# Fused gated-recurrence and feed-forward kernel: first groups of two blocks, one more y transpose by DMA, last output split at column 288, new instruction orders

## The chip, the cores and the metric

The kernel runs on one core of one Trainium2 chip. The metric is the device time of one execution in microseconds. Ten runs of the kernel before gave a median of 182.35 us, from 181.86 to 183.18.

## What is computed

Two stages follow each other. The first is a gated linear recurrence for 4 batches, 8 heads, 768 steps and a head width of 48; its output is laid out as 3072 tokens of 384 values. The second is a feed-forward layer with 2048 hidden values and a squared ReLU.

```python
for t in range(S):
    state = alpha[:, :, t, :, None] * state + np.einsum('bhd,bhe->bhde', k[:, :, t], v[:, :, t])
    y[:, :, t] = np.einsum('bhd,bhde->bhe', q[:, :, t], state)
x = y.transpose(0, 2, 1, 3).reshape(B * S, H * D)
r = np.maximum(x @ w_in, 0.0)
out = (s * (r * r) + b) @ w_out
```

Inputs and output are float32; the kernel multiplies in bfloat16 and accumulates in float32.

## The kernel before

**Blocks.** The tokens are cut into 24 blocks of 128 steps, six for each batch. Within a block the recurrence is written as matrix products. The logarithm of alpha is summed over the steps on TensorE ("cum", L533 for blocks 0 to 5, L766 for later ones), and its exponentials scale q and k (exp on ScalarE, L558 or L781; products on VectorE, L601 and L609, or L801). The scaled q and k are transposed: blocks 0 to 12 on TensorE (L619, L812) with a copy out of PSUM (L629 and L631, L822 and L824), later ones by a DMA transpose (L827). The transposed q and k give the products A of queries with keys (L711), which a mask on VectorE makes causal (L725). "KV" products of k and v (L647, L835) feed the running state: VectorE adds (L679), GpSimd multiplies by the block's decay (L686, `st_snew`); for block 0 ScalarE copies the product first (L673, `st_scopy`). Block y is the sum of state and q (L742) and of masked A and v (L750); ScalarE takes it out of PSUM (L848).

Blocks 0 to 5 are worked as three pairs with the two steps of a pair of rows side by side (`pair_ops`, L1024); for pairs 0 and 1 a selection product on TensorE brings v into order (L577, copies L588 and L590), for pair 2 four DMAs do (L596). Later blocks are worked one by one (`block_ops`, L1125). v is cast to bfloat16 by ScalarE or GpSimd, as lists at the top of the file say (L571 or L573, L796 or L798).

**Feed-forward.** y is transposed, on TensorE (L853) with a copy (L865, L867) or by a DMA transpose (L870), and the blocks are gathered in groups by `GROUPS`. For every group, `mm1` (L884) multiplies the transposed y by w_in, always into a full bank of 128 x 512 values: four column blocks of the hidden layer for a group of one block, two for a group of two, one for a group of four. ScalarE takes the ReLU (L900), VectorE squares (L912). `mm2` (L919) multiplies the squares by w_out, four products to an operation, sixteen to a block of the output. The output is scaled by s and gets its bias from VectorE in one operation (L934), for the first six blocks from ScalarE and GpSimd (L951, L958), and is stored from SP's queue (L945). The last block's output is worked in two halves of columns, each with its own products, evacuation and store (`half_of`, L914). w_in and w_out arrive in quarters of 768 KB in four buffers, which they share (L442, L456), and are cast in halves by GpSimd or ScalarE (L451 and L453, L465 and L467); w_out's quarter waits until w_in's has been cast.

**The order.** No engine's order follows the program text. Every operation is recorded with a duration and its dependencies (`op`, L131), and `ORDER` holds a list of operation numbers for each engine, which were found by a search beforehand. `Schedule.run` (L156) goes through these lists with the recorded durations, gives out the six PSUM banks on the way and yields begin times; `emit` (L240) writes the operations in this order of time. It also puts dummy products on zeros (L1201) ahead of a TensorE operation that is planned to come after a gap, in the first 36 us. The planner lets GpSimd and VectorE begin after their constants:

```python
free = {e: {"POOL": 6.9, "DVE": 4.5}.get(e, 0.7) for e in engines}
```

The engines run their lists strictly in order, so an operation that waits holds all that stand behind it on its engine. Loads and stores all go through SP's queue, in SP's order.

Of the kernel before, what the change touches and what calls it, by code (L numbers as in the profile page):

```python
# [13 lines left out]
GROUPS = [1, 1, 2, 2, 2, 4, 2, 2, 2, 2, 4]  # L14
# [6 lines left out]
POOL_CASTS = [0, 1, 2, 5, 6]  # L21
CASTP = -400.0
W_HW = True
WIN_CASTS = [0, 1, 2, 5, 6]
A2 = [0, 1, 2, 5, 8, 9, 10]
POOL_V = [2]
ACT_V1 = [6, 8, 9, 13, 15, 17, 22, 23]
ACT_T1 = [7, 8]
DVE_VC = [3]
DVE_YC = [2, 3, 4, 7, 10, 13]  # L30
NIN = 4
PE_T = [6, 7, 8, 9, 10, 11, 12]
PE_Y = [7, 8, 9, 10, 11, 13]
# [3 lines left out]
ACT_T = [2, 3]  # L37
# [3 lines left out]
NOUT = 4  # L41

# [4 lines left out]
        31 35 32 33 34 36 37 38 0 3 6 9 39 12 41 16 42 40 21 43 26 47 213 45 52 44 353 46 375  # L47
        397 49 48 50 354 355 356 51 377 413 376 378 510 298 414 399 398 415 400 587 512 114 530
        416 513 663 511 607 532 533 589 590 678 531 736 133 609 610 541 588 666 210 665 608 598
        203 618 826 750 680 529 679 811 738 664 739 275 282 689 752 674 753 871 681 346 851 626  # L50
        737 606 814 352 813 751 497 491 747 761 828 829 699 853 694 854 827 812 852 873 503 837
        822 872 774 509 862 769 882 580 874 845 586 850 870 887 656 735 662 804 729 810 941 947
        959 953 965
    """,
    "POOL": """
        81 1 2 4 83 8 158 10 14 160 13 17 212 23 27 232 303 53 310 368 113 390 405 412 421 202
        518 209 132 595 274 544 601 281 621 671 744 677 758 764 819 834 825 840 865
    """,
    "ACT": """
        57 134 66 67 68 69 144 146 70 147 58 143 145 60 62 80 135 153 155 87 93 137 89 95 5 7 97  # L60
        164 11 100 103 211 170 116 106 122 219 217 221 119 174 218 220 125 180 18 177 186 183
        192 22 283 189 28 285 195 299 286 301 112 236 131 242 302 357 287 379 244 359 360 401
        382 381 249 246 403 404 307 201 208 255 361 252 261 297 365 417 258 314 383 267 420 419
        514 372 264 517 321 374 318 516 327 591 324 394 273 534 330 593 594 333 536 537 396 429
        339 435 611 667 336 437 538 614 669 613 670 442 682 439 448 445 528 740 280 451 454 615
        457 685 460 742 743 684 463 548 466 469 472 475 478 830 754 481 605 484 625 832 815 757
        555 756 833 552 818 561 817 558 567 564 875 573 686 693 855 698 570 857 858 631 628 877
        634 637 640 878 643 646 773 649 859 768 704 701 710 707 716 713 722 719 849 844 779 879
        869 776 785 782 886 788 791 794 797 889 892 895 898 901 904 907 910 913 916 919 922 925
        928 931 934  # L70
    """,
    "DVE": """
        71 72 73 74 76 149 78 150 148 151 91 85 90 82 139 168 162 167 157 98 159 101 104 166 117
        172 107 123 15 120 175 225 126 224 181 178 223 187 222 229 19 184 231 227 20 190 234 239
        193 240 289 288 24 196 238 25 291 29 293 305 304 295 250 247 30 362 54 363 309 256 312
        253 385 262 384 367 56 370 316 389 259 387 268 422 407 265 406 322 423 392 319 409 425
        411 325 520 328 427 433 432 334 331 519 524 431 540 340 522 337 597 543 526 443 440 539
        600 449 446 617 452 455 620 596 546 458 673 461 616 464 467 676 351 345 550 603 470 473
        476 623 479 687 688 485 482 672 746 496 556 490 749 553 760 562 559 568 696 691 565 695
        574 763 502 745 508 821 632 571 759 629 824 635 579 638 641 585 836 644 771 770 766 861  # L80
        647 839 650 835 705 820 864 702 711 860 708 881 655 717 714 880 842 846 847 720 661 723
        867 780 884 728 777 786 783 789 792 795 734 798 890 893 896 899 902 905 908 911 809 914
        917 920 923 926 929 932 803 935 940 958 946 952 964
    """,
    "PE": """
        63 64 65 141 142 140 75 77 59 61 79 84 152 154 138 86 92 161 136 88 94 156 96 163 99 102
        115 169 165 105 121 171 215 216 214 118 173 176 124 179 108 182 185 191 109 228 127 128
        230 226 188 129 284 194 233 110 111 130 300 197 235 198 241 204 237 205 290 206 243 292
        358 199 380 294 248 245 402 200 306 207 308 296 254 311 251 260 364 366 257 55 313 266
        369 418 386 315 388 263 269 371 515 270 320 373 391 317 271 326 408 424 323 410 393 272  # L90
        329 592 426 332 535 276 277 395 428 338 523 434 335 430 278 436 521 612 668 279 441 542
        525 438 444 599 447 341 527 342 450 683 453 741 343 456 344 619 459 545 347 348 462 465
        547 349 675 350 549 471 468 602 477 474 492 480 604 622 486 483 831 487 755 624 493 488
        554 551 494 495 489 816 498 748 560 499 557 500 566 563 690 504 505 572 506 762 692 501
# [171 lines left out]
def kernel(  # L266
# [22 lines left out]
    d_model = moe_w_in.shape[0]  # L289
# [584 lines left out]
    for g, m in enumerate(GROUPS):  # L874
# [3 lines left out]
        for tt in range(m):  # L878
            n = len(quads) // 4
# [34 lines left out]
    def half_of(x):  # L914
        n, h = quads[x][3:]
# [324 lines left out]
```

## Time and profile before

| what | value |
|---|---|
| median of ten runs | 182.35 us |
| profiled execution, device time | 181.97 us |
| its span from first to last instruction | 180.2 us |
| granted TensorE clock, mean | 1.000 |
| DMA to landing, last store | 1.6 us after its issue at 177.28 |
| moved by DMA | 34.44 MB, mean 191 GB/s |

PE is TensorE, PEld its weight loads, DVE VectorE, ACT ScalarE, POOL GpSimd and SP the engine that issues DMAs. In the list of groups each line has the source line, the engine, the operation, its tiles and shapes, how often it occurs, the busy time, the mean duration in ns, and the engine's idle time before it with what ended it:

```profile
L900 ACT ACTIVATE r<-bank 128x512 bf16<-128x512 f32 x96 | 55.6, 599 | 33.3 <-PE bank L891 23.1
L891 PE MATMUL bank<-xd,w_in_bf 128*128 128x256 bf16 (+2 forms) x528 | 73.2, 282 | 0.1
L924 PE MATMUL bank<-w_out_bf,gt 128*128 128x384 bf16 (+1 forms) x400 | 73.0, 319 | 0.0
```

Products are pipelined, so the mean duration of one is longer than the distance from one to the next: the 282 ns of an L891 product contain the run through the array, while a row of six with 256 columns takes 0.66 us in the chain. A timeline line begins with the start and the length in us, and can merge several instructions (x12). The chain of work that ended last is followed back from the last instruction, at each step to what released it.

### The profile page before, as it was taken

To read this page: it belongs to the slowest core of one execution; us is meant where nothing else is said; L and a number is where in the kernel's file an instruction comes from. 1 tells how busy PE (TensorE), PEld (TensorE's weight loads), DVE (VectorE), ACT (ScalarE), POOL (GpSimd) and SP (SyncE) were. 2 spreads that over 40 slices of the span, in tenths; PEclk is the share of its full clock that TensorE was granted. 3 is DMA by queue.
4 is the path that set the end of the run, shared out by engine and by line. 5 is a ranking of instruction groups with operands and counts; after the bars stand their busy time and mean duration, and the time that the engine had idled before them with its cause. 6 is when DMAs were issued, how large, how long until landed. Compare 5 with 4: busy or idle time off the path is not lost.

```text
span 180.2 us, 4618 instructions
## 1 busy us (share of the span) xinstructions
PE 171.8 (95%) x1789; PEld 121.3 (67%) x1789; DVE 135.5 (75%) x250; ACT 116.2 (64%) x247; POOL 51.5 (29%) x96
## 2 busy tenths in 40 slices
PE   6888789999999999999999999999999999999992
PEld 4565778766778787755546677776877787444671
DVE  6489569999999999997796489478976954555332
ACT  3887788769899779978737756544554266557200
POOL 7823847250124429265400122204220000000000
PEclk9999999999999999999999999999999999999999
DMA  6999999979895999998969999878887742200331
GB/s 154 324 350 377 377 353 262 329 162 228 174 176 113 223 200 215 200 201 187 196 141 196 213 218 214 205 184 176 172 206 181 153 105 78 89 0 0 135 109 65
DMA packets 111909, 34.44 MB, mean 191 GB/s; under 512 B 104848, under 2 KB 110352, under 8 KB 111888
## 3 DMA queue, kind: packets, MB, share of 16 engines
q1 hardware_dynamic: 111888, 34.16, 79.7%
q8 instruction: 14, 0.23, 0.5%
q14 instruction: 7, 0.06, 0.1%
HBM read 25.17 MB, written 4.72 MB: 166 GB/s over the span
## 4 chain that ended last, share of the span: by engine, by line
PE 75%; DVE 6%; DMA 6%; SPq 6%; ACT 4%; issue 1%; ACTq 0%
PE bank L924 32%; PE bank L891 29%; DMA wst<-in_moe_w_in_dram 6%; SPq L415 4%; DVE gt L912 3%; PE a_ps L711 3%; PE bank L750 2%; ACT r L900 2%; PE bank L812 2%; PE bank L742 2%; PE bank L766 2%; PE bank L835 1%; SPq L442 1%; DVE qk L609 1%; DVE colsum L470 1%
## 5 line engine op out<-in xcount | busy, mean ns | idle before, releaser
L900 ACT ACTIVATE r<-bank 128x512 bf16<-128x512 f32 x96 | 55.6, 599 | 33.3 <-PE bank L891 23.1
L891 PE MATMUL bank<-xd,w_in_bf 128*128 128x256 bf16 (+2 forms) x528 | 73.2, 282 | 0.1
L924 PE MATMUL bank<-w_out_bf,gt 128*128 128x384 bf16 (+1 forms) x400 | 73.0, 319 | 0.0
L912 DVE TENSOR_TENSOR gt<-r 128x512 bf16<-128x512 bf16 x96 | 45.2, 481 | 18.0 <-ACT r L900 17.5
L891 PEld LDWEIGHTS <-w_in_bf 128*128 128x128 bf16 x528 | 46.0, 98 | 15.5 <-issue 0.2
L924 PEld LDWEIGHTS <-gt 128*128 128x128 bf16 x400 | 36.4, 97 | 19.4 <-issue 0.2
L686 POOL TENSOR_TENSOR s_st<-t,blast 64x192 bf16<-64x192 bf16 x32 | 18.9, 591 | 20.7 <-DVE t L679 13.7
L934 DVE SCALAR_TENSOR_TENSOR o_sb<-bank,s_col,bias_w 128x384 f32<-128x384 f32 (+1 forms) x19 | 11.2, 592 | 10.1 <-PE bank L924 6.8
L725 DVE TENSOR_TENSOR am<-a_ps,mask_one 128x1024 bf16<-128x1024 f32 x14 | 17.0, 1216 | 2.3 <-PE a_ps L711 2.3
L798 POOL CAST vb<-v_in 128x384 bf16<-128x384 f32 x10 | 5.8, 576 | 42.3 <-DMA v_in<-in_v_dram 15.7
L848 ACT ACTIVATE yn<-bank 128x384 bf16<-128x384 f32 x24 | 11.7, 492 | 8.2 <-PE bank L750 8.2
L801 DVE TENSOR_TENSOR qk<-q_in,b_s 128x384 bf16<-128x384 f32 x18 | 11.9, 660 | 3.5 <-DMA q_in<-in_q_dram 3.5
L801 DVE TENSOR_TENSOR qk<-k_in,binv 128x384 bf16<-128x384 f32 x18 | 10.8, 601 | 1.0 <-DMA k_in<-in_k_dram 0.9
L679 DVE TENSOR_TENSOR t<-bank,s_st 128x384 bf16<-128x384 f32 x16 | 8.8, 547 | 1.8 <-POOL s_st L686 1.1
L759 ACT ACTIVATE la<-a_in 128x384 bf16<-128x384 f32 x18 | 9.3, 531 | 0.4 <-DMA a_in<-in_alpha_dram 0.4
L781 ACT ACTIVATE binv<-bank 128x384 f32<-128x384 f32 x18 | 9.0, 498 | 0.9 <-PE bank L771 0.9
L781 ACT ACTIVATE b_s<-bank 128x384 f32<-128x384 f32 x18 | 8.8, 499 | 0.0
L742 PE MATMUL bank<-s_st,qkT 128*128 128x96 bf16 x80 | 6.7, 206 | 1.1 <-POOL s_st L686 0.9
L750 PEld LDWEIGHTS <-am 128*128 128x128 bf16 x192 | 7.1, 96 | 0.9 <-DVE am L725 0.7
L465 POOL CAST w_out_bf<-wst 128x768 bf16<-128x768 f32 x5 | 5.2, 1032 | 8.7 <-DMA wst<-in_moe_w_out_dram 8.6
L711 PEld LDWEIGHTS <-qkT 64*128 64x128 bf16 x192 | 5.4, 94 | 2.9 <-issue 2.1
L742 PEld LDWEIGHTS <-qkT 128*128 128x128 bf16 x80 | 5.0, 98 | 3.0 <-issue 1.2
(90 smaller groups left out, 188.8 us busy)
## 6 DMA issues: line engine op xcount, KB each, us to landing
out_dram<-o_sb SPq DMA_DIRECT2D x23, 192.0 KB, 2.3
a_in<-in_alpha_dram SPq DMA_DIRECT2D x18, 192.0 KB, 3.8
k_in<-in_k_dram SPq DMA_DIRECT2D x18, 192.0 KB, 3.6
q_in<-in_q_dram SPq DMA_DIRECT2D x18, 192.0 KB, 3.9
v_in<-in_v_dram SPq DMA_DIRECT2D x18, 192.0 KB, 3.9
wst<-in_moe_w_in_dram SPq DMA_DIRECT2D x4, 768.0 KB, 8.6
wst<-in_moe_w_out_dram SPq DMA_DIRECT2D x4, 768.0 KB, 8.6
a_in<-in_alpha_dram SPq DMA_DIRECT2D x3, 384.0 KB, 4.1
```

The costliest lines, as they stand in the source:

```text
L686: nc.gpsimd.tensor_tensor(out=s_sb[n % 4][rows, :, cols], in0=(scratch() if n in ACT_S else t1_sb[n % 2])[rows, :, cols], in1=blast(n)[row ...
L711: nc.tensor.matmul(out=a_of(n, e)[:, p, :], lhsT=T[rows, 1, p], rhs=T[rows, 0, p], start=True, stop=True,)
L725: nc.vector.tensor_tensor(out=dst, in0=src, in1=mk.unsqueeze(1).to_broadcast([128, dst.shape[1], 128]), op=ALU.mult,)
L742: nc.tensor.matmul(out=y_of(n)[:, 96 * p : 96 * p + 96], lhsT=qT[:, p], rhs=s_sb[(n - 1) % 4][:, p, :], start=(p == 0), stop=False,)
L781: nc.scalar.activation(out=(binv_sb if inv else b_sb)[n // 2 % 2][:, n % 2].rearrange("a h d -> a (h d)"), in_=cb[:, 0 : H * D], func=AF.E ...
L801: nc.vector.tensor_tensor(out=qk1_of(n)[:, x, :, 0:D], in0=block_in((q_in, k_in)[x], n), in1=(b_sb, binv_sb)[x][n // 2 % 2][:, n % 2], op= ...
L848: nc.scalar.activation(out=yn_sb[n // 2 % 2][:, n % 2], in_=y_of(n), func=AF.Copy)
L891: nc.tensor.matmul(out=hp[:, i * n : (i + 1) * n], lhsT=w_in_bf[:, kk, 128 * j : 128 * (j + 1)], rhs=xd_sb[g % 3][:, kk, 0:n], start=(kk = ...
L900: nc.scalar.activation(out=r_sb[w % 2], in_=bank("h", w), func=AF.Relu)
L912: nc.vector.tensor_tensor(out=dst, in0=r, in1=r, op=ALU.mult)
L924: nc.tensor.matmul(out=bank("o", i)[:, cols], lhsT=gt_sb[:, slot, j, :], rhs=w_out_bf[:, j, cols], start=(j == 0), stop=(j == NJ - 1),)
L934: nc.vector.scalar_tensor_tensor(out=out_sb[i % NOUT][:, cols], in0=bank("o", i)[:, cols], scalar=s_col, in1=bias_w[:, cols], op0=ALU.mult ...
```

## The change

- `GROUPS` begins with a group of two blocks in place of two groups of one: blocks 0 and 1 are now worked together in the feed-forward layer, with products of 256 columns in place of twice as many of 128.
- Block 13 leaves `PE_Y`: its y is transposed by DMA and no longer on TensorE.
- The last block's output is split at column 288 (`LAST`) in place of 192.
- Which engine does some of the casts and copies is changed in eight lists. Among them v of pair 0 is cast by GpSimd in place of ScalarE, and v of pair 2 by ScalarE in place of GpSimd.
- Some recorded durations are set anew, above all of the A products (0.43 to 0.335, and 0.66 to 0.56 for two blocks together). They move nothing by themselves but enter into the planner's begin times.
- All five lists of `ORDER` are new. In SP's list v of pair 0 comes third and q fifth, and alpha of pair 2 stands between the first and second quarter of w_in. In GpSimd's list the cast of v and the first three state updates stand ahead of the casts of w_in. In TensorE's list the selection of v and the KV products of pair 0 stand ahead of its transposes. At the end, the first 288 columns of block 23 are finished among block 22's products, and the last sixteen products are those of its 96 columns.

One line is added, so line numbers from 45 on are one higher than before.

```diff
-GROUPS = [1, 1, 2, 2, 2, 4, 2, 2, 2, 2, 4]
+GROUPS = [2, 2, 2, 2, 4, 2, 2, 2, 2, 4]
-POOL_CASTS = [0, 1, 2, 5, 6]
+POOL_CASTS = [0, 1, 2, 6]
-WIN_CASTS = [0, 1, 2, 5, 6]
+WIN_CASTS = [1, 3, 4, 5, 7]
-POOL_V = [2]
-ACT_V1 = [6, 8, 9, 13, 15, 17, 22, 23]
-ACT_T1 = [7, 8]
-DVE_VC = [3]
-DVE_YC = [2, 3, 4, 7, 10, 13]
+POOL_V = [0]
+ACT_V1 = [6, 9, 10, 12, 15, 16, 17, 18, 21, 22]
+ACT_T1 = [7, 8, 11, 12]
+DVE_VC = [2]
+DVE_YC = [1, 2, 3, 5, 10, 11]
-PE_Y = [7, 8, 9, 10, 11, 13]
+PE_Y = [7, 8, 9, 10, 11]
-ACT_T = [2, 3]
+ACT_T = [1, 3]
+LAST = 288
...
-        cols = slice(0, d_model) if h is None else slice(h * d_model // 2, (h + 1) * d_model // 2)
+        cols = slice(0, d_model) if h is None else (slice(0, LAST), slice(LAST, d_model))[h]
...
-        op("PE", 0.66, t, st_A2, n, r=qkT, w=["a"] + ab, lat=0.27, take=ab, blk=n)
+        op("PE", 0.56, t, st_A2, n, r=qkT, w=["a"] + ab, lat=0.27, take=ab, blk=n)
...
-            op("PE", 0.65 if h is None else 0.34, t, mm2, x,
+            op("PE", {None: 0.65, 0: 0.5, 1: 0.18}[h], t, mm2, x,
...
-                    op("DVE", 0.535 if h is None else 0.33, t + 0.1, oevac, x, r=[o, "bias", ("col", 1)],
+                    op("DVE", {None: 0.535, 0: 0.43, 1: 0.23}[h], t + 0.1, oevac, x, r=[o, "bias", ("col", 1)],
```

## The prediction

> **What bounds the kernel now.** I read the page's busy time and chain first, then the busy time by stage, then the timeline of the first 24 us, and last the end.
>
> ```profile
> PE 171.8 (95%) x1789; PEld 121.3 (67%) x1789; DVE 135.5 (75%) x250; ACT 116.2 (64%) x247; POOL 51.5 (29%) x96
> ...
> PE 75%; DVE 6%; DMA 6%; SPq 6%; ACT 4%; issue 1%; ACTq 0%
> ```
>
> ```profile
> 0.00:10.00 10.00, 7.86 (x53) 5.30 (x54) 5.47 (x14) 6.53 (x13) 7.32 (x33) 1.00 0.92 247
> 10.00:20.00 10.00, 7.88 (x138) 5.56 (x136) 9.00 (x15) 7.48 (x14) 4.79 (x7) 1.00 1.07 374
> ...
> 60.00:100.00 40.00, 40.00 (x434) 26.58 (x432) 35.85 (x65) 30.44 (x71) 14.89 (x20) 1.00 0.97 195
> ```
>
> (Columns: stage, its length, busy time of PE, PEld, DVE, ACT, POOL.) From 60 us on PE is busy in every microsecond, and from 24 us to the end the list of who waited for whom shows no wait of PE for another engine. So two things set the time: how much PE work there is, and when PE gets into this unbroken run. The other engines have 4 to 25 us to spare in 60 to 100 us. The head is where PE waits:
>
> ```profile
> 7.32 1.49 POOL L327 MEMSET s_st<- 128x384 bf16 x4
> ...
> 8.03 0.85 PE L1201 MATMUL bank<-zeros_bf 128*128 128x256 bf16 x3
> ...
> 8.67 1.72 PE L619 MATMUL bank<-ident_bf,qk 128*128 128x128 bf16 x16
> ...
> 8.98 0.84 ACT L573 ACTIVATE vb<-v_in 128x768 bf16<-128x768 f32 x1
> ...
> 11.58 0.40 PE L711 MATMUL a_ps<-qkT 64*128 64x128 bf16 x8
> ...
> 17.36 0.49 PE L1201 MATMUL bank<-zeros_bf 128*128 128x256 bf16 x3
> ...
> 18.23 0.84 PE L891 MATMUL bank<-xd,w_in_bf 128*128 128x128 bf16 x12
> ...
> 20.35 2.17 PE L891 MATMUL bank<-xd,w_in_bf 128*128 128x128 bf16 x36
> ```
>
> POOL is occupied by constants until 8.81. The same three dummy products take 0.85 at 8 us and 0.49 at 17 us: PE runs at half speed at first, and the clock record turns to full at 10.06. The end:
>
> ```profile
> 167.00 9.80 PE bank L924 x76
> ...
> 176.83 0.42 DVE o_sb L934
> ```
>
> The last store is issued at 177.28 and lands 1.6 later; the span ends at 180.2.
>
> **The change, part by part.** The sum is made against the profiled execution (span 180.2, device time 181.97, so 1.8 lie around the span). The median is 182.35, which is 0.38 more; I add that at the end.
>
> *PE work.* In the chain 12 first products (L891) of 128 columns take 0.67 (56 ns each), six of 256 columns 0.66 (109 ns). Two groups of one block are 96 x 56 = 5.38 us; one group of two is 48 x 109 = 5.23. Gain 0.15, on PE's path. ReLU and square count stay at 8 for these blocks.
>
> *y transpose of block 13.* PE loses 3 transposes of 56 ns: gain 0.17. A DVE copy (0.35) goes. SP gets one DMA transpose more, 2.8 from issue to landing (issue list). It lies 60 us before the end and is consumed a group later, under PE's unbroken work. SP waits for block 13's y there, and the loads behind it in SP's queue wait too; such waits cost SP up to 2.2 now without PE waiting. I take 0 (0 to 0.5).
>
> *Engine choices* (v casts, T copies, y copies between ACT, DVE, POOL; the casts of weights). Two T copies more on ACT (1.03 instead of DVE's 0.68), two v casts more (0.53). After 60 us ACT has 9.6 of 40 to spare. I take 0 (-0.3 to 0.5): a gain is possible, since a changed order can also lose the small gaps around L711.
>
> *Last output.* PE work is equal: 32 x 82 ns = 2.6 for 192 columns; 16 of 288 and 16 of 96 by the same width rule (162 ns for 384, 42 ns for the 96 columns of L742) are 16 x 122 + 16 x 42 = 2.6. The last evacuation shrinks: rows of 0.61 for 384 and 0.42 for 192 columns give about 0.32 for 96, gain 0.10. But block 22's last product moves from 0.98 before PE's end to 0.67 before it, so its 192 KB store goes out just ahead of the last one. That store now lands 1.85 after issue: PE's end + 1.85, and the last one behind it at about + 2.1, where it is today (178.90 - 176.79 = 2.11). I take -0.05 (-0.15 to +0.2). The Trainium skill (DMA: Bandwidth & Descriptors, Specifications) asks for at least 512 B per run, below which the engine reads and rewrites; the new store has 384 B rows. The row against it: 104848 of 111909 packets are already under 512 B, and slices with them move 350 to 377 GB/s. By the rule the 48 KB could move at half rate, still under 0.2; by the row it costs nothing. I follow the row.
>
> *The head* is the large term, and it goes both ways. The order shows that v of pair 0 is loaded third instead of fifth (landing at about 6.5 instead of 8.96), and cast by POOL, not ACT; q of pair 0 moves to fifth. On PE the selection product of v (L577) and KV (L647) now stand ahead of the transposes (L619). The planner lets POOL begin at 6.9 (line 170), but the trace has it free at 8.81. So the cast is 8.81 + 1.11 (the L571 row) = 9.92, no earlier than today's 8.98 + 0.84, and now PE's transposes, which start at 8.67 today, queue behind it. Step by step, with today's durations at full clock:
> - v product 10.05, two dummies, KV at 10.6, k transposes at 11.1, their copy on ACT (1.01; behind a v copy, an exp and the KV copy) ends 13.1: A products start at 13.2, today 11.58.
> - DVE now has the state sum (L679), which waits for POOL's first state (KV copy to 12.1, then 1.47: 13.65), and both q products ahead of the masks: masks at 14.8, done 14.8 + 0.68 + 0.68 + 1.21 = 17.4, today 15.6.
> - POOL's third state needs a sum behind those masks (17.95), then 1.2, and only then POOL casts w_in (0.85): 20.0. The other way in, A products of pair 1 at 18.7, transpose, copy, is 20.1. First products start at 20.2.
> - From there PE goes on: two units 1.31, block 3's y, a unit, a wait of 0.4 for block 2's mask (DVE 22.9), y, then three units, transposes and cumulative sums of pair 2: six of eight units done at 26.2. w2 and w3 (landing 21.2 and 23.3, one 1.2 us load later than today because pair 2's alpha goes between) are cast in time.
>
> Of the moved loads, one has a wait that grows: w_out's first quarter goes into the buffer of w_in's first (L456), so SP holds it until POOL's cast at 20.0, and k of pair 2 and the other quarters stand behind it (today it is issued at 16.38). The queue is filled to 24.5 by then (w3 at 23.3, q of pair 2 1.2 more), so this costs 0; were the cast later than about 22, each microsecond would delay w_out by one, and from 33 us PE's second products with it.
>
> Today at 24.04 PE has done 55 of 96 products. To equal that later point it lacks 41 x 0.056 = 2.30, a y transpose 0.17, pair 2's sums 0.85, less the two units (1.31) that the new kernel still owes: 2.01, and 0.1 of waits. It is there at 26.15. So at full clock the head is +0.05 (the 0.15 included).
>
> But the clock: with v's product waiting, PE has nothing from about 8.1 to 10.05. Today it is busy from 5.09 and goes to full at 10.06. The Trainium skill (TensorE: Matmul & The Clock Gate, The HAM clock gate) says that half rate ends after a busy, free-running window of 3.4 us. By the row alone (full at 10.06 in any case) nothing is added. By the rule the gap spoils that window and the next ends at 13.5: v 0.64, dummies 0.43, KV 0.7, k transposes 0.86, q transposes 0.86 give copies done at 14.3 and masks at 15.95 instead of 14.8: +1.1. I take the rule, since today's switch came only after five busy microseconds. The dummies cannot help, they stand behind the same wait. About 0.2 of it is won back, as today's waits between 30 and 38 us on late w_out are met later.
>
> Sum: 0.05 + 1.1 - 0.2 - 0.17 - 0.05 = +0.7: 182.7 profiled, median 183.1.
>
> **Rivals.**
> (1) The clock turns full anyway near 10: -0.2, 182.2. For it: the window's phase is free, and one dense stretch (5.09 to 8.1) remains. Against it: 3 us are less than the window.
> (2) The head gains. One mechanism, at POOL: state updates stand ahead of the weight casts. Today the second state starts at 18.84 behind three casts, and PE waits until 19.98 for it; in the new order it can start at 14.3. If my mask chain is 1.5 too late (the planner's copies overlapping better), first products start near 18.7, PE then runs through and is at the equal point at 24.7: -1.45 - 0.2, 180.7. Decisive is the first L891: before 19.2 this wins. Up to 20.1 it ends below 182.
> (3) A second wait follows: nine units run nearly back to back from 26 us (0.65 each) and ACT has ReLUs of 0.60 plus exps and two w_out casts in one place; or v of pair 2, landing at about 37 instead of 30, holds block 4's y through its DMA (42.5, needed 43). Another +1.0: 184.1.
>
> **How the numbers follow.** Half clock case 0.40 (182.5 to 183.7), (1) 0.28 (181.7 to 182.7), (2) 0.20 (180.5 to 181.7), (3) 0.12 (183.7 to 184.6). A measurement tells about 0.3% (0.55 us) from no change. Faster: (2) and the low end of (1), 0.26; same 0.28; slower 0.46. The range leaves out the lower half of (2) and the top of (3): 181.2 to 184.2.
>
> **What would show it.** Dummies or v products near 10 us at half duration mean (1); the A products (L712 in the new numbering) at 13 to 14.5 and the first L892 at 20 to 21.5 mean my head; before 19.2 means (2). PE waits after 26 us mean (3). The last store landing 2.1 after PE's end confirms the end. I am wrong altogether if PE waits beyond 60 us, which nothing in the trace suggests.

## The result, and the profile after

The changed kernel took 181.16 us (median of 15 runs, 180.82 to 182.0) beside 182.59 us (50 runs) for the kernel before on the same chip: a ratio of 0.9926, 95% interval 0.9907 to 0.9945. It is faster, where I had forecast 183.1 and slower. Three more measurements beside other runs gave 0.9945 (0.9916 to 0.9973), 0.9953 (0.9913 to 0.9992) and 0.9942 (0.9903 to 0.9981), so the gain is 0.9 to 1.35 us. The profiled execution has a device time of 180.85 and a span of 178.8 (181.97 and 180.2 before). Three of the other profiles used below (`a_again_2`, `a_alpha_late`, `a_by_block`) caught an execution of the longer kind, and are compared only with one another, up to 36 us.

Page after, busy time and the chain's shares:

```profile
PE 170.4 (95%) x1740; PEld 119.7 (67%) x1740; DVE 132.8 (74%) x248; ACT 117.9 (66%) x251; POOL 48.8 (27%) x93
...
PE 83%; DMA 5%; POOL 4%; DVE 2%; ACT 2%; issue 1%; SPq 0%; POOLq 0%; DVEq 0%
```

PE holds 83% of the chain instead of 75%: less of the time is spent in steps of other engines. By stage, after (columns as in the prediction; the granted clock is third from the end):

```profile
0.00:10.00 10.00, 5.48 (x41) 3.57 (x42) 5.00 (x13) 5.71 (x11) 8.17 (x34) 1.00 0.91 247
10.00:20.00 10.00, 9.41 (x142) 7.25 (x140) 8.36 (x17) 7.98 (x15) 4.31 (x8) 0.83 1.09 373
20.00:24.00 4.00, 4.00 (x57) 3.58 (x55) 3.88 (x8) 4.00 (x9) 2.81 (x4) 1.00 1.09 366
...
30.00:36.00 6.00, 6.00 (x62) 4.33 (x60) 5.97 (x11) 4.89 (x9) 1.69 (x2) 1.00 0.88 252
...
60.00:100.00 40.00, 40.00 (x408) 26.53 (x406) 31.73 (x60) 32.70 (x78) 13.97 (x20) 1.00 1.01 196
```

The same view of the kernel before, two stages that the prediction did not show:

```profile
20.00:24.00 4.00, 3.40 (x70) 3.31 (x70) 1.97 (x5) 3.60 (x7) 2.81 (x4) 1.00 1.11 357
...
30.00:36.00 6.00, 5.92 (x58) 4.31 (x57) 6.00 (x12) 4.67 (x9) 2.05 (x3) 1.00 1.03 310
```

PE is busy for less of the first ten microseconds than before (5.48 against 7.86), the clock falls to 0.83 on average between 10 and 20 us, and yet from 20 to 42 us PE has no idle slice; before it stood still for 0.60 us of the 4 from 20 to 24. PE's timeline after, in the head:

```profile
7.13 0.38 PE L1202 MATMUL bank<-zeros_bf 128*128 128x256 bf16 x2
9.69 0.48 PE L578 MATMUL bank<-vb,sel_bf 128*128 128x384 bf16 x2 [2.18 <-POOL vb L572]
...
10.77 1.73 PE L620 MATMUL bank<-ident_bf,qk 128*128 128x128 bf16 x16
...
13.93 0.61 PE L712 MATMUL a_ps<-qkT 64*128 64x128 bf16 x8
...
19.89 1.47 PE L892 MATMUL bank<-xd,w_in_bf 128*128 128x256 bf16 x12
```

The wait for v behind GpSimd's constants is there (2.18 us), and so is a stretch at half clock: it runs from 10.99 to 14.40. The end (last steps of the chain, then the timeline):

```profile
165.87 9.80 PE bank L925 x76
175.70 0.32 DVE o_sb L935
```

```profile
174.82 0.84 PE L925 MATMUL bank<-w_out_bf,gt 128*128 128x96 bf16 x16
...
175.66 0.81 SPq L946 DMA_DIRECT2D out_dram<-o_sb  x2
```

PE ends at 175.66 in place of 176.79. The last store lands 2.09 later (2.11 before).

**Where the time went.** For each moment T, I subtract from T the work that PE has done by then, every product counted with its usual distance to the next at full clock (56 ns for 128 columns, 109 for 256, and so on; dummies count nothing). The rest is time lost. It was taken up to 36 us, where the traces agree in their records; further on up to 1.2 us of products are missing from some of them.

| profile | full clock from | first L891/L892 | lost by 20 | by 24 | by 36 |
|---|---|---|---|---|---|
| before | 10.06 | 18.23 | 11.20 | 11.93 | 12.71 |
| after | 4.16, half 10.99 to 14.40 | 19.89 | 11.38 | 11.43 | 11.40 |

Of the 1.31 us by 36 us, 0.50 are there at 24 us and 0.81 come between 24 and 36. The tail adds nothing: from PE's end to the end of the device time it is 5.18 us before and 5.19 after.

**After 36 us a part is lost again.** PE ends 1.13 us earlier, and its work is 0.31 us less (161.27 and 160.96 us, counted with the same distances), so that only 0.82 us less are lost at its end. The difference goes between 42 and 60 us, where PE loses 0.94 before and 1.64 after. The largest waits there after are 0.34 at 52.45, 0.25 at 59.7 for a DMA transpose of y, and 0.16 at 54.0 for a cast of v. The first stands behind a product of VectorE that waits for a k landing at 51.34. After:

```profile
51.36 0.56 DVE L802 TENSOR_TENSOR qk<-k_in,binv 128x384 bf16<-128x384 f32 x1 [0.63 <-DMA k_in<-in_k_dram]
...
52.45 0.62 PE L813 MATMUL bank<-ident_bf,qk 128*128 128x128 bf16 x8
```

Before, VectorE waits for no load there:

```profile
52.85 0.64 DVE L801 TENSOR_TENSOR qk<-k_in,binv 128x384 bf16<-128x384 f32 x1
```

### The profile page after: what moved, and what is told of

It is laid out like the page before. It is cut to its first block, busy times and chain, and to the rows that moved or that the text cites. A ratio compares the mean times of both kernels' runs of the same rounds, so it can differ in the third digit from the quotient of the medians.

```text
span 178.8 us, 4509 instructions
## 1 busy us (share of the span) xinstructions
PE 170.4 (95%) x1740; PEld 119.7 (67%) x1740; DVE 132.8 (74%) x248; ACT 117.9 (66%) x251; POOL 48.8 (27%) x93
## 3 DMA queue, kind: packets, MB, share of 16 engines
HBM read 25.17 MB, written 4.72 MB: 167 GB/s over the span
## 4 chain that ended last, share of the span: by engine, by line
PE 83%; DMA 5%; POOL 4%; DVE 2%; ACT 2%; issue 1%; SPq 0%; POOLq 0%; DVEq 0%
PE bank L925 34%; PE bank L892 33%; PE a_ps L712 3%; DMA xd<-yn 3%; DMA a_in<-in_alpha_dram 2%; PE bank L751 2%; PE bank L620 2%; PE bank L743 2%; PE bank L767 1%; PE bank L836 1%; PE bank L813 1%; PE bank L854 1%; PE bank L712 1%; DVE am L726 1%; PE bank L578 1%
## 5 line engine op out<-in xcount | busy, mean ns | idle before, releaser
L892 PE MATMUL bank<-xd,w_in_bf 128*128 128x256 bf16 (+1 forms) x480 | 72.0, 294 | 0.1
L925 PE MATMUL bank<-w_out_bf,gt 128*128 128x384 bf16 (+2 forms) x400 | 71.1, 319 | 0.0
L892 PEld LDWEIGHTS <-w_in_bf 128*128 128x128 bf16 x480 | 44.5, 97 | 15.2 <-DMA xd<-yn 0.2
L687 POOL TENSOR_TENSOR s_st<-t,blast 64x192 bf16<-64x192 bf16 x32 | 19.7, 616 | 43.5 <-DVE t L680 40.6
L935 DVE SCALAR_TENSOR_TENSOR o_sb<-bank,s_col,bias_w 128x384 f32<-128x384 f32 (+2 forms) x19 | 11.2, 592 | 9.9 <-PE bank L925 9.3
L799 POOL CAST vb<-v_in 128x384 bf16<-128x384 f32 x8 | 4.6, 580 | 37.0 <-DMA v_in<-in_v_dram 29.8
L802 DVE TENSOR_TENSOR qk<-k_in,binv 128x384 bf16<-128x384 f32 x18 | 9.8, 550 | 1.0 <-DMA k_in<-in_k_dram 1.0
L712 PE MATMUL a_ps<-qkT 64*128 64x128 bf16 x136 | 7.0, 224 | 0.3 <-DVE qkT L632 0.3
L751 PE MATMUL bank<-vb,am 128*128 128x48 bf16 x144 | 6.5, 183 | 0.0
```

Of the source, the lines that this page charges most:

```text
L687: nc.gpsimd.tensor_tensor(out=s_sb[n % 4][rows, :, cols], in0=(scratch() if n in ACT_S else t1_sb[n % 2])[rows, :, cols], in1=blast(n)[row ...
L712: nc.tensor.matmul(out=a_of(n, e)[:, p, :], lhsT=T[rows, 1, p], rhs=T[rows, 0, p], start=True, stop=True,)
L751: nc.tensor.matmul(out=y_of(n)[:, 48 * h : 48 * h + 48], lhsT=am_sb[n % 2][:, h % 2, h // 2, :], rhs=v[:, 48 * h : 48 * h + 48], start=(h ...
L802: nc.vector.tensor_tensor(out=qk1_of(n)[:, x, :, 0:D], in0=block_in((q_in, k_in)[x], n), in1=(b_sb, binv_sb)[x][n // 2 % 2][:, n % 2], op= ...
L892: nc.tensor.matmul(out=hp[:, i * n : (i + 1) * n], lhsT=w_in_bf[:, kk, 128 * j : 128 * (j + 1)], rhs=xd_sb[g % 3][:, kk, 0:n], start=(kk = ...
L925: nc.tensor.matmul(out=bank("o", i)[:, cols], lhsT=gt_sb[:, slot, j, :], rhs=w_out_bf[:, j, cols], start=(j == 0), stop=(j == NJ - 1),)
```

## The experiments

The theory after the first comparison: the new head is no shorter, but PE no longer waits after it; state updates stand ahead of weight casts on GpSimd, and the products ask for w_in's quarters when they are there. The rival: the gain comes from the parts named in the change (groups of two, the split, the y transpose). The transpose of block 13 alone was not run: its 0.17 us are below what a measurement can tell. The eight lists of engine choices were not run apart from the orders either. In the edits below, operation names stand for the numbers in `ORDER`.

**The named parts.** `a_last192` undoes the split, `b_last288` makes it alone, `a_groups11` puts back the groups of one block in the new order.

```diff
-LAST = 288
+LAST = 192
```


> The changed kernel with the last output split at column 192 again, in its own order. Order theory: the split brings nothing, within 0.1 of the changed kernel, ratio 0.992 to 0.993, last store landing about 2.1 us after PE's last product. Tail theory (the 0.25 us by which the time from PE's last product to the end of the span shrank, 3.41 to 3.16, is the split's): 0.2 to 0.3 slower, ratio 0.994.

```diff
-        cols = slice(0, d_model) if h is None else slice(h * d_model // 2, (h + 1) * d_model // 2)
+        cols = slice(0, d_model) if h is None else (slice(0, 288), slice(288, d_model))[h]
```


> The kernel before with the last output split at column 288, and nothing else. Order theory: within 0.1 of the kernel before, ratio 0.999 to 1.001. Tail theory: 0.2 to 0.3 faster, ratio 0.9985, with the time from PE's last product to the end at 3.1 to 3.2 us.

```diff
-GROUPS = [2, 2, 2, 2, 4, 2, 2, 2, 2, 4]
+GROUPS = [1, 1, 2, 2, 2, 4, 2, 2, 2, 2, 4]
...
+    def rx(w):
+        return w // 4 if w < 8 else w % 2
...
-        nc.scalar.activation(out=r_sb[w % 2], in_=bank("h", w), func=AF.Relu)
+        nc.scalar.activation(out=r_sb[rx(w)], in_=bank("h", w), func=AF.Relu)
```


> The changed kernel with the groups of one block put back (blocks 0 and 1 each in a group of their own, 96 products of 128 columns for 48 of 256), in the changed kernel's orders; ReLUs alternate between two buffers as before. Order theory (the gain of 1.4 us comes from the new orders, which give PE other work while it used to wait between 20 and 42 us): 0.15 to 0.3 slower than the changed kernel, so ratio to the kernel before about 0.994, and PE's waits stay gone. Group theory (the group of two itself brings most of it): 0.8 to 1.3 slower, ratio 0.997 to 1.0. First L892-kind product near 19.9 us in both.

Measured against the kernel before: `a_last192` 1.0018 (0.998 to 1.0055), `b_last288` 1.0042 (1.0006 to 1.0079), `a_groups11` 1.0012 (0.9984 to 1.0040). The unaltered kernel had not been run on that chip, which left open whether a part or the chip took the gain. So it was run again (`a_again`), with the groups once more beside it.

> The changed kernel once more, unaltered, as the measure for the others of this call. If the gain of 0.7% belongs to the order, the ratio is 0.990 to 0.995 here too. The rival: on the chip of the experiments so far the changed kernel has no gain at all (they all gave 1.000 to 1.004 although only small parts were undone), because late DMA landings between 36 and 160 us take it away; then 0.998 to 1.003.

> The changed kernel with blocks 0 and 1 as groups of one again, beside the unaltered one. By the prediction's term it is 0.15 us slower than the unaltered one (ratios differ by 0.001). Rival: groups of two are what makes the head denser, since the six column blocks need half the weight loads; then 0.5 us or more slower, visible between 20 and 30 us in time lost by TensorE.

`a_again` 0.9945, `a_groups11_2` 0.9962 (0.9922 to 1.0002): 0.3 us apart within intervals of twice that. The profiles are sharper. From PE's end to the span's end `a_last192` takes 3.17 us and the profile after 3.16; `b_last288` takes 3.53 and the kernel before 3.41. In the profiles the split is worth nothing (`a_last192` was not timed beside the unaltered kernel); for `b_last288`'s 1.0042, whose interval just leaves out 1, these 0.12 us are all that the end can have cost. Both profiles with groups of one lose as little between 20 and 36 us (0.14 and 0.22) as the groups of two. None of the named parts carries the gain alone. Groups of two and the y transpose account for the 0.31 us of work that PE saves; the rest is in the orders together with the lists of engine choices.

**GpSimd's order.** In the changed kernel, w_in's casts were put back ahead of the second and third state update:

```diff
 POOL
-st_vcast 0; st_snew 0; st_snew 1; st_snew 2; cast 0 1; cast 1 1; cast 2 0
+st_vcast 0; st_snew 0; cast 0 1; cast 1 1; st_snew 1; cast 2 0; cast 2 1; st_snew 2
```


> The changed kernel with one thing of GpSimd's order put back: the first two casts of w_in ahead of the second state update, the next two ahead of the third, as the kernel before had it. If the states ahead of the casts are what the gain rests on: the second state waits for the cast of w_in's second quarter (landing 19.3), ends near 21.3 instead of 15.6, y of block 1 and the first first-layer product move from 19.9 to about 22.5 us, 1.0 to 2.0 slower than the changed kernel, ratio 0.998 to 1.003. If the head has slack because the weights bound it (w_in's last quarter is cast at 24.4 in any case): under 0.5 slower, ratio below 0.995.

Ratio 1.0178 (1.0143 to 1.0213, six executions), 1.6% above those of `a_last192` and `a_groups11` on the same chip. GpSimd's timeline in this run:

```profile
15.28 0.83 POOL L452 CAST w_in_bf<-wst 128x768 bf16<-128x768 f32 x1 [2.46 <-DMA wst<-in_moe_w_in_dram]
19.66 0.83 POOL L452 CAST w_in_bf<-wst 128x768 bf16<-128x768 f32 x1 [3.55 <-DMA wst<-in_moe_w_in_dram]
20.45 1.08 POOL L687 TENSOR_TENSOR s_st<-t,blast 64x192 bf16<-64x192 bf16 x2
```

For 3.55 us GpSimd waits for a quarter of weights while the state update behind it, ready since about 14, holds the recurrence: the first L892 comes at 24.86, and PE has lost 16.73 by 36 us. State ahead of casts is necessary in this order. It does not follow that the old order had the same fault to the same degree, so that was tried there:

```diff
 POOL, kernel before
-cast 0 1; cast 1 0; st_snew 1
+cast 0 1; st_snew 1; cast 1 0
 ACT, kernel before
-cast 3 1; relu 1; relu 2
+relu 1; cast 3 1; relu 2
```

`b_state_first` makes the first of these moves, `b_castlate` the second, `b_two_moves` both.

> The kernel before with one instruction moved: ScalarE's cast of w_in's last quarter (which waits for its landing at 22.08) stands behind one more ReLU. Theory: the gain of the changed kernel between 20 and 24 us comes from this wait of TensorE, 0.76 us at 22.70, alone; then the wait shrinks to under 0.2 and the profile has TensorE ahead by about 0.5 at 24 us, and the time is 0.2 to 0.6 us shorter (ratio 0.997 to 0.999), less than 0.76 because w_out's landings at 33 us still hold the second products. Rival: the squares or w_out take the wait over at once; then under 0.1 us and ratio 1.000.

> The kernel before with one instruction moved: GpSimd's second state update (L686, today 18.84 to 19.92) stands ahead of the w_in cast at 18.05, into the 1.7 us in which GpSimd waits for that quarter; its sum is ready at 16.07. Theory: the changed kernel's gain between 18 and 24 us comes from its states standing ahead of the casts. Then TensorE's wait of 0.90 at 19.07 shrinks to under 0.2, the products of L891 go on at once, and TensorE is 0.4 to 0.9 us ahead at 24 us; the time falls by 0.3 to 0.8 us (ratio 0.9955 to 0.9985). Rival: the next wait (for a PSUM bank and ScalarE's ReLU behind the cast of w_in's last quarter, landing 22.08) grows by what this one loses; then 0.2 us or less at 24 us.

> The kernel before with both moves: the second state update ahead of the w_in cast, and ScalarE's cast of w_in's last quarter behind one more ReLU. Theory: the two waits between 18 and 24 us (0.90 and 0.60) hold each other up, so that each move alone brings little and both together about 1.0 us at 24 us in time lost by TensorE. If w_out's quarters, which land at 33.4 and 37.8 in the kernel before and at 32.0 and 35.1 in the changed one, do not take it back, the time falls by 0.7 to 1.2 us (ratio 0.993 to 0.996), which is the whole gain of the changed kernel. Rival: w_out takes it back between 30 and 42 us; then the lead at 24 us is there and that at 42 us is under 0.4.

Measured: 0.9988 (0.9956 to 1.002), 0.9995 (0.9961 to 1.0029), 0.9996 (0.9964 to 1.0028). The theory in this form fell. The two waits of the kernel before, in the list of who waited for whom:

```profile
PE bank L742 <- POOL s_st L686: 0.9, 1, 0.9
PE bank L853 <- ACT r L900: 0.6, 1, 0.6
```

PE in the run with both moves:

```profile
19.34 0.33 PE L742 MATMUL bank<-s_st,qkT 128*128 128x96 bf16 x4
19.51 0.36 PE L750 MATMUL bank<-vt,am 128*128 128x48 bf16 x8
19.72 0.83 PE L891 MATMUL bank<-xd,w_in_bf 128*128 128x128 bf16 x12
21.31 1.51 PE L891 MATMUL bank<-xd,w_in_bf 128*128 128x128 bf16 x24 [0.76 <-ACT w_in_bf L453]
```

Both waits are gone, and a new one of 0.76 stands in their place, for the cast of w_in's third quarter. The old order reaches its products before their weights have landed (its quarters land at 18.0, 20.0 and 22.1); whatever is taken from a wait for a state becomes a wait for weights.

**Asking for the weights later.** `b_fill` adds a move to these two: block 1's first unit, which needs the first quarter only, ahead of block 0's third.

```diff
 PE, ACT and DVE, kernel before with both moves
-unit 0; unit 1; unit 2; unit 4
+unit 0; unit 1; unit 4; unit 2
```


> The kernel before with the two moves of the earlier run and one more: block 1's first product unit, which needs only w_in's first quarter, stands on TensorE, ScalarE and VectorE ahead of block 0's third, which waits for the cast of the third quarter (wait of 0.76 at 20.55). That ReLU gets a buffer of its own (three in place of two). Theory: what TensorE loses in the old order between 18 and 24 us is that it has reached the products before their weights; with other work in that place 0.4 to 0.7 us more are won at 24 us. Whether the time follows depends on w_out: if the quarters that land at 33.4 and 37.6 hold TensorE, the lead is gone at 42 us and the ratio stays at 0.998 to 1.001; if not, it is 0.994 to 0.997.

Ratio 0.9955 (0.9924 to 0.9985), but its profile shows no lead: 12.10 lost by 24 us, 13.15 by 36. A wait of 0.63 at 21.46 for a ReLU has taken the place of that for the weights. The time spoke for the theory and the trace did not; I count this one as inconclusive. The opposite was cleaner: `a_by_block` is the run with groups of one in the new order, but with block 1's third quarter ahead of block 0's first, as the kernel before does it.

```diff
-units 4 0 5 1 6 2 7 3   (quarters 0 0 1 1 2 2 3 3)
+units 4 5 6 0 7 1 2 3   (quarters 0 1 2 0 3 1 2 3)
```


> The changed kernel with groups of one block for blocks 0 and 1, as in the earlier run with such groups, but the eight units of products in the order of the kernel before: the one block's third quarter ahead of the other block's first, so that w_in's last quarter is asked for by the fifth unit and not by the seventh. Theory: the order in which blocks share a quarter of weights is what keeps TensorE from waiting on weights in the changed kernel (groups of two do it by their shape). Then it loses 0.5 to 1.2 us between 20 and 28 us, against 0.1 to 0.2 in the run with groups of one in the new order, and the time is 0.3 to 0.9 us longer than that kernel's. Rival: state updates ahead of the casts carry it alone; then the loss stays under 0.3 us.

PE in this run, then GpSimd:

```profile
22.18 0.60 PE L1207 MATMUL bank<-zeros_bf 128*128 128x256 bf16 x4
22.62 0.50 PE L892 MATMUL bank<-xd,w_in_bf 128*128 128x128 bf16 x6
23.30 0.51 PE L892 MATMUL bank<-xd,w_in_bf 128*128 128x128 bf16 x6 [0.18 <-POOL w_in_bf L452]
```

```profile
21.64 1.60 POOL L452 CAST w_in_bf<-wst 128x768 bf16<-128x768 f32 x2 [0.57 <-DMA wst<-in_moe_w_in_dram]
```

The planner fills the foreseen wait with four dummies (L1207), and the product behind them still waits 0.18 for GpSimd's cast of the third quarter. Between 20 and 28 us this kernel loses 1.31 us, where `a_again_2`, with the same clock, loses 0.02. The time is 0.9982 (0.995 to 1.0015): about 0.7 us above the changed kernel's on other chips, although its interval reaches that of `a_groups11_2`. That the order of the units against the landings is worth about a microsecond of PE's time is shown by the profile; the time agrees without proving it.

**Loads.** Two parts of SP's new order were undone in the changed kernel: v of pair 2 ahead of w_out's third quarter (`a_v2_early`), and alpha of pair 2 behind w_in (`a_alpha_late`, with its logarithm, cumulative sums and exponentials later on PE, ACT and DVE).

```diff
 SP
-w_out 1; w_out 2; s; w_out 3; v of pair 2
+w_out 1; v of pair 2; w_out 2; s; w_out 3
```


> The changed kernel with one load moved back in SP's list: v of pair 2 stands ahead of w_out's third quarter again, as in the kernel before. Theory: the 0.8 to 1.2 us that TensorE loses between 24 and 36 us in all four looks at the old order, and not in the new one, are waits for w_out's quarters behind that load (they land 1.4 and 2.8 us later there). Then the third and fourth quarter land 1.0 to 1.2 us later here, TensorE loses 0.4 to 1.0 us between 28 and 42 us, and the time is 0.3 to 0.8 us longer than the unaltered kernel's. Rival: the new order of TensorE's products, not the load, carries it; then the loss stays under 0.2 us.

```diff
 SP
-w_in 0; alpha of pair 2; w_in 1; w_in 2; w_in 3
+w_in 0; w_in 1; w_in 2; w_in 3; alpha of pair 2
```


> The changed kernel with one part of its load order undone: alpha of pair 2 is loaded behind w_in's four quarters again, as in the kernel before, and its logarithm, cumulative sums, exponentials and q products stand behind the sixth unit of products. Theory: at 24 us the new order has 0.4 to 0.7 us more cumulative sums done than the old one, and equally many first products; the early alpha gives TensorE work that needs no weights while w_in's last quarters are still on the way. Then TensorE loses 0.4 to 0.8 us between 20 and 28 us here (0.02 to 0.6 in the new order so far), although those quarters land 1.2 us earlier. Rival: the weights that come 1.2 us earlier give it the same amount of other work, and it loses under 0.3 us there.

`a_v2_early`: 0.995 (0.991 to 0.999). w_out's last two quarters land at 33.42 and 35.73, 1.4 and 0.6 later than in the profile after, and PE loses 0.12 between 24 and 36 us: the rival held, this load carries nothing. `a_alpha_late`: 1.0014 (0.9979 to 1.0049): no gain is left, although the unaltered kernel was not run on that chip. PE has lost only 0.15 more between 20 and 24 us, so that in this window the earlier weights do make up for it; then come 1.8 by 36:

```profile
25.46 1.15 PE L1202 MATMUL bank<-zeros_bf 128*128 128x256 bf16 x9
27.06 0.81 PE L534 MATMUL bank<-la,U_bf 128*128 128x384 bf16 x4 [0.46 <-ACT la L526]
```

ScalarE's logarithm, which lands in its queue behind a cast and two ReLUs, is done at 27.0, and PE stands behind its dummies for it. Part of this is where I put the logarithm, so the run shows that alpha's chain would be the next wait in the new order, not that it is what the old order lost.

**The clock.** The profiles of the changed kernel differed from one another already in the head. `a_zeros_dve` clears the state buffers on VectorE, so that v's cast can begin earlier; `a_dummies` adds five dummies in PE's gap.

```diff
-    s_sb = many("s_st", 4, [128, NP, 96], BF16, zero=nc.gpsimd)
+    s_sb = many("s_st", 4, [128, NP, 96], BF16, zero=nc.vector)
```


> The changed kernel with the four state buffers cleared by VectorE, so that GpSimd is free about 1.3 us earlier. Theory: GpSimd's constants gate the cast of v and with it TensorE's wait of 2.2 us and the whole head; the cast begins near 7.5 to 8.4 instead of 8.61, the first L892 comes up to 1 us earlier, and the time falls by 0.3 to 0.8 us against the unaltered kernel. Rival: the landings of w_in's last quarter (23.57) and of w_out hold TensorE afterwards, or VectorE's own constants come late, and the gain is under 0.1.

```diff
                     warm(max(0.0, begin[i] - last - 0.4) / cold)
+                    if self.ops[i][3].__name__ == "st_V" and self.ops[i][4] == (0, 1):
+                        warm(0.7)
```


> The changed kernel with five more dummy products ahead of v's selection product, in TensorE's gap from 7.5 or 8.7 to 9.7 us. Theory: without a long gap half clock does not come back or stay after 10 us, as in the three profiles of the kernel before (full from 9.39 to 10.35): k's sixteen transposes take 1.07 us and not 1.5 to 1.9, the first L892 is at 19.2 or earlier in the profile, and the time is 0.2 to 0.6 us below the unaltered kernel of this call. Rival: the later landings of w_in's last quarters (21.4, 23.6) absorb what the head gains and the ratio equals that of the unaltered kernel within 0.001; or at half clock the five products (0.21 us each) reach past 9.7 and delay the head by 0.1 to 0.3 us.

> The changed kernel a third time, for the clock. Four profiled executions of its head so far: full clock from 9.09 us on (first L892 at 19.14), half clock from 10.99 to 14.40 (19.89), and, in kernels whose head is the same, half clock up to about 13.4 twice (20.61 and 20.67). Theory: TensorE's gap of 1 to 2.2 us ahead of v's product lets the clock of the next 3 us fall out differently from execution to execution; the first L892 comes at 19.1, 19.9 or 20.6. The ratio is 0.991 to 0.997. Rival: the clock is a matter of the chip and this execution looks like the last.

> The kernel with five more dummy products in TensorE's gap once more: it had the lowest time so far (ratio 0.9928, interval 0.9887 to 0.9968) with full clock from 4.17 us to the end in its profile. Theory: the shorter gap keeps the clock full or lets it turn full by 10.5, so the first L892 is at 19.2 again. Rival: the earlier look was luck, and half clock between 10 and 14 us shows here too, with the first L892 at 19.8 or later and a ratio equal to the unaltered kernel's.

> The changed kernel a fourth time, beside the next ones. Ratio 0.991 to 0.997; the start of full clock is again open (it was 9.09, 12.58, and 14.40 after an earlier stretch), and the first L892 follows it: 19.1 if full before 10, 20.2 to 20.6 if full after 12.5.

| profile | full clock from | first L891/L892 | lost by 20 | by 24 | by 36 |
|---|---|---|---|---|---|
| old head: `b_last288` | 9.39 | 18.93 | 11.24 | 12.38 | 13.21 |
| `b_castlate` | 10.35 | 18.39 | 11.24 | 12.15 | 13.10 |
| `b_state_first` | 8.20 | 18.59 | 10.48 | 12.10 | 13.32 |
| `b_two_moves` | 4.21 | 18.66 | 10.55 | 11.83 | 12.84 |
| `b_fill` | 9.23 | 18.91 | 10.82 | 12.10 | 13.15 |
| new head: `a_again` | 9.09 | 19.14 | 10.71 | 11.30 | 11.38 |
| `a_again_2` | 12.58 | 20.23 | 11.75 | 11.74 | 12.03 |
| `a_again_3` | 8.44 | 19.06 | 10.61 | 10.84 | 10.89 |
| `a_last192` | about 13.4 | 20.61 | 12.07 | 12.18 | 12.20 |
| `a_groups11` | 13.37 | 20.67 | 12.07 | 12.22 | 12.21 |
| `a_groups11_2` | 4.72 | 19.15 | 10.71 | 10.84 | 10.93 |
| `a_v2_early` | 12.92 | 20.43 | 11.91 | 11.90 | 12.03 |
| `a_alpha_late` | 12.58 | 20.23 | 11.91 | 12.06 | 13.88 |
| `a_by_block` | 12.86 | 20.41 | 11.91 | 12.83 | 13.51 |
| gap altered: `a_zeros_dve` | 10.00 | 18.72 | 10.28 | 10.87 | 10.89 |
| `a_dummies` | 4.17 | 19.13 | 10.73 | 10.76 | 10.92 |
| `a_dummies_2` | 8.87 | 20.78 | 12.24 | 12.34 | 12.52 |

The same instructions at full clock, in `a_again`:

```profile
9.78 0.48 PE L578 MATMUL bank<-vb,sel_bf 128*128 128x384 bf16 x2 [1.01 <-POOL vb L572]
...
10.86 1.07 PE L620 MATMUL bank<-ident_bf,qk 128*128 128x128 bf16 x16
...
12.78 0.40 PE L712 MATMUL a_ps<-qkT 64*128 64x128 bf16 x8
```

The sixteen transposes take 1.07 here and 1.73 after. With PE's gap left as it is (0.97 to 2.18 us ahead of v's product), full clock came to stay by 9.1 us in three of eleven profiles and after 12.5 us in eight (`a_pool_casts_first` too: half from 10.77 to 14.18). Where that gap was under 0.5 us, in the six profiles with the old head, in `a_zeros_dve` and in `a_dummies_2`, full clock was there by 10.4 in all eight. `a_dummies` fits neither group: its gap is still 1.57 us, and it kept full clock from 4.17 on. So the gap goes with a late clock, but its length alone does not decide.

The records let one read what else does. The stretches of full and half clock that end inside the span are whole multiples of 3.41 us (3.41, 6.83, 163.84, 170.67 and others). Cut each profile into steps of 3.41 us on that grid, and take PE's idle time in each step of the first 17 us. Half clock turned to full after steps with at most 0.71 us idle and stayed half after steps with 0.44 or more. Full clock was lost after the two steps with 2.11 us idle (`after`, `a_pool_casts_first`) and kept over 1.57 (`a_dummies`) and 1.64 (`a_groups11_2`). The grid lies differently from one execution to the next, so the same gap falls into one step or is shared by two. This is a reading of 19 profiles; no run moved the grid, and between 0.44 and 0.71 it does not tell the outcomes apart. (`a_last192` has no record; its 13.4 is taken from its products.)

The first L892 is at 19.1 with full clock and at 20.35 on average without (seven profiles with GpSimd's new order): 1.2 us. But this difference does not last. PE's transposes L813 of the same three blocks begin at:

| profile | clock | first L892 | near 44 | near 53 | near 74 |
|---|---|---|---|---|---|
| `a_again_3` | full | 19.06 | 43.34 | 52.55 | 73.86 |
| `a_again` | full | 19.14 | 43.92 | 52.74 | 74.02 |
| `a_groups11_2` | full | 19.15 | 43.58 | 52.88 | 73.78 |
| after | half | 19.89 | 43.79 | 52.45 | 73.58 |
| `a_v2_early` | half | 20.43 | 44.33 | 52.80 | 73.87 |
| `a_last192` | half | 20.61 | 45.03 | 53.73 | 75.78 |
| `a_groups11` | half | 20.67 | 44.81 | 53.28 | 73.99 |

Near 74 us six of the seven are within 0.44 us of one another, where their heads were 1.6 apart, and the profiled execution, with half clock, is ahead of all (`a_last192` is not: PE waits 0.8 in it near 72 for a logarithm). The load of k that the transposes near 53 need lands between 51.34 and 52.37 in all seven, and VectorE waits for it 0.57 to 1.00 us in the three with full clock, 0.18 to 0.63 in the four without. Why these loads come no earlier was not tested.

The times: `a_zeros_dve` 0.9965 (0.9925 to 1.0005), `a_dummies` 0.9928 (0.9887 to 0.9968) beside `a_again_2`'s 0.9953, `a_dummies_2` 0.9927 (0.9887 to 0.9967) beside `a_again_3`'s 0.9942. `a_zeros_dve` starts v's product at 8.63 and its first L892 at 18.72, and then meets the weights; its rival held:

```profile
23.13 0.83 PE L892 MATMUL bank<-xd,w_in_bf 128*128 128x256 bf16 x6 [0.40 <-POOL w_in_bf L452]
```

With five dummies the clock was full in time in both profiles. The second one's first L892 is late (20.78) for another reason, v of pair 1, for whose cast PE waits 0.94 at 14.6. `a_dummies` is 0.2% below the unaltered kernel both times, and beats the kernel before; that it beats the changed kernel lies within the intervals and is not shown, and its transposes near 74 us (73.75) begin no earlier than those of the profile after.

## Why the prediction was wrong

The prediction's sum was +0.7; the profiled execution is 1.12 shorter. The steps that failed are the chain through the head, the clock's term as an addition to the end, and the waits between 24 and 60 us.

- **The clock, "+1.1: I take the rule".** The mechanism and the size at the first products were right: half clock after the gap, 1.2 us. Rule and row both had a part: the prediction's case (1) (full near 10) is three of eleven executions. What failed is the addition of the 1.1 to the end of the kernel. The executions with and without half clock meet again by 74 us (73.58 after, 74.02 and 73.86 for the same kernel with full clock), and those that come early wait longer for a load near 52 us.
- **The chain through the head, "First products start at 20.2" at full clock.** This failed, by 1.1 us: it was 19.06 to 19.15. Term by term, against `a_again`: v's product 10.05, was 9.78; A products 13.2, was 12.78; masks 14.8 to 17.4, were 14.13 to 16.54; GpSimd's first cast of w_in 19.15, was 18.21. For one of its parts the cause can be seen: VectorE's rows give 0.55 for a product or a sum, but one follows the other after 0.46 or 0.47, and I had added durations where distances count. Some eight operations of VectorE stand in a row there, which makes about 0.6 of the 1.1; 0.27 more were there at v's product, and the rest is not resolved. At half clock the 21.3 of the sum were 20.35. This is the decisive point that rival (2) had named, "before 19.2 this wins. Up to 20.1 it ends below 182": 19.89 and 180.85 in the profiled execution.
- **"So at full clock the head is +0.05", the comparison at 24 us.** It failed with the chain: at full clock the new head has lost 0.63 to 1.09 less by 24 us than the kernel before, at half clock after the gap (the profiled one) 0.50 less.
- **"About 0.2 of it is won back" after that.** It failed as well: between 24 and 36 us the kernel before loses 0.78 us (0.8 to 1.2 in all six profiles with its order), the changed one nothing (0.2 or less in most, 0.3 at most, leaving out the two runs whose edits put waits there, `a_alpha_late` and `a_by_block`). I had read "no wait of PE for another engine" from 24 us on from a list that shows waits of some tenths only, while several of 0.1 to 0.2 us stood between its products. The largest two before 36 us, 0.24 near 30.7 and 0.17 near 33.4, are waits for ReLUs; the prediction's late w_out shows only behind them, with 0.14 near 39.4 for a cast. Which of the changed orders removes them stays open: v of pair 2 does not, and groups of two do not.
- **PE's way from 42 us on, taken as unbroken.** It is not: between 42 and 60 us the new order loses 0.7 us more than the old one. The prediction put this stretch at nothing; here the failure makes the gain smaller than the head's.
- **What held.** PE's work shrank by the forecast 0.15 and 0.17. The split is worth nothing (PE's end to landing 2.09, was 2.11), 384 B rows cost nothing against before (the last 48 KB landed 1.66 after issue, the 96 KB before 1.62), though with half the bytes in the same time this does not show that they move at full rate. PE's wait for v behind GpSimd's constants was there (2.18). w_out's first quarter was held by GpSimd's cast, and nothing came of it. The DMA transpose of block 13's y kept PE waiting nowhere: after 61 us the profile after has no wait of PE over 0.15 us.
- **Rival (3)** did not come: no wait of its kind after 26 us. Rival (2) did, with its place right and its reason in part: the first products are not earlier than before (19.89 against 18.23); the gain is that up to 42 us nothing has to be waited for after them. That its 180.7 lies near the 180.85 is therefore in part luck.

## What to carry to other kernels

A start that comes earlier is worth nothing if it is earlier than its data: compare the time of each first use with the landing of what it uses, and order the units so that each quarter of weights serves all blocks before the next is asked for. Removing one wait in such a stretch only shows the next; the sum to make is what PE has done by a moment at which everything has landed. Follow a gain or a loss of the head to the end in the same way: here 1.2 us of clock were gone 50 us later. When adding up a chain on one engine, take the distance from start to start in the timeline, not the durations.

## What the hardware showed unexpectedly

After a gap of 1.0 to 2.2 us on TensorE near 9 us it was at half clock until 12.6 to 14.4 us in eight of eleven executions and not in the other three, with the same instructions up to there; half clock could come back after a full stretch (full from 4.16, half from 10.99 for 3.41 us, after 2.11 us idle in one step of 3.41). With half clock in the head or with full clock, six of seven profiles came to the same place, within 0.44 us, 50 us later. DMA transposes do not take the same time from one execution to the next: in `a_groups11` one issue took 2.07 us where most take 1.2, and PE stood still until it had landed:

```profile
127.57 2.07 SPq L828 DMA_TRANSPOSE qkT<-qk  x1
...
129.41 0.40 PE L712 MATMUL a_ps<-qkT 64*128 64x128 bf16 x8 [0.85 <-DMA qkT<-qk]
```

Such waits, of 0.3 to 1.4 us, stood at different places in most of the later profiles with the new order, and in one with the old (`b_two_moves`, 0.9 at 117). Executions of one kernel were up to 4 us apart there (181.66 to 185.45 for `a_again`); that these waits are the reason was not tested.
